# GFNet mixing and SoLU on one core: the opening's first step in the place of x, unit 0 from SBUF to SBUF, the tables' issues in another order

## The chip, the core and the metric

The program runs on one core of a Trainium2 chip. A core has a matrix engine (PE, with its weight loads shown as PEld), a vector engine (DVE), a scalar engine (ACT), a general engine (POOL) and a sequencer that only issues transfers and waits (SP). Transfers (DMAs) are issued by SP, ACT or POOL and carried by 16 DMA engines between DRAM and the on-chip memory (SBUF, 128 partitions). Products land in PSUM. The metric is the time of one execution on the device in microseconds (us).

## What is computed

The reference has two parts. Eight samples of 3136 tokens with 256 channels are filtered along the tokens in the frequency domain, and the result goes through a gated layer:

```python
X = np.fft.rfft(x, axis=1)
Y = X * (filt_r + 1j * filt_i)[None, :, :]
y = np.fft.irfft(Y, n=3136, axis=1)            # (8, 3136, 256)
h = y.reshape(25088, 256) @ w_in               # (25088, 1024)
sm = softmax(h); solu = h * sm                 # with 1e-9 in the denominator
ln = (solu - mean) / sqrt(var + 1e-6) * g_ln
out = ln @ w_out                               # (25088, 256)
```

The weights w_in and w_out arrive as 64-bit floats and are converted on the chip.

## The kernel before, in words

**The transform.** 3136 = 49 x 64. A sample goes through four steps. The *first step* (`Spectrum.first`, L204) multiplies x, as 98 rows (49 rows and their mirror images) by 32 positions by 256 channels, with a table of 98 x 100: 8 pieces of 4 positions, four matmuls each, copied out of PSUM by ACT (L213) and stored to DRAM (`d1`, L166 and L167: 96 rows on one queue, the last 4 rows on the other). The 100 result rows are 25 residues by 4 parts. The *forward step* (`forward`, L242) takes them back with residues along the free axis: 7 units of four residues (two pairs), the last of one. `fetch` (L226, L229) reads a unit of 512 KB from d1. Per unit PE makes `pb`, DVE multiplies with the filter (`multiply`, L260 to L262: two products and a sum for the real part on DVE, two products on DVE and the sum on POOL for the imaginary part), PE makes `pc` (`inverse`, L267), ACT copies it to `g` (L277) and `store` (L281) puts it to DRAM (`d2`). The *back step* (`fetch_back`, `back`, L285 to L304) reads d2 in 8 pieces `t4`, multiplies (`py`) and copies to `y`, which holds two samples' worth of tokens.

**The opening** (L307 to L490) does sample 0 alone and converts the weights. Its pools are: `fp` for the tables and filters, `t1` (two buffers of 4 KB in each partition), `r` (32 KB, one buffer: all of x of sample 0, later all of t4), `t2` (two of 4 KB), `p`, `g` and `wp` (raw weights, three of 4 KB, and `power`, two of 2 KB). Results of the first step go to t1 for pieces 0 and 1 and to spare places in `y` for pieces 2 to 7; units 1 to 6 are later fetched to the same spare places, unit 0 to t2. `load_tables(i0, n, dma)` (L361) issues nine transfers: a table `de` (L363) and eight parts of the filters `f` (L366). `begin(j)` (L391, L316) issues the load of raw weights j of 8, on POOL. `idle` (L426) is a matmul whose result nobody reads; eight of them stand in PE's order between the first step and the first forward step, and they read the first tables and filters.

**The conversion** (`load_float64`, L321) of one eighth of the weights: DVE makes eight instructions (L328 to L341), ACT one multiply (L330), POOL a product and a sum (L342, L343).

**What sets the order.** Within a `manual_schedule` block each engine works in the order in which the program emits its instructions. The opening is one such block and the main loop another; instructions emitted outside them (the x loads of the second sample's pieces 6 and 7, L776, called at L813) are placed by the scheduler when their memory is free. Before the change the opening's issues are: SP: x pieces 0 to 7 of the first half (one, one, two, two, two pieces at a time, row 48 apart), the four-row stores, fetches of units 0 to 2, tables of pairs 4 to 7, fetches of units 3 and 4, tables of pairs 8 to 12, fetches of units 5 and 6, then t4, x of the second sample, and the filters' copy to DRAM (L478). POOL: the second half of x, raw weights 0 and 1, tables of pairs 0 to 3, then its halves of conversions 0 and 1. ACT: the stores of the first step and of the units.

**After the opening** new pools take the memory of the opening's pools from the same start: wk2 (36 KB), fp1 (8), up (22), hp (16), wk (5), sp (4), r1 (12: x and t4 of later samples), t1 (6), t2, p, g, de1. The main loop (L819, `step`) runs over 196 blocks of 128 tokens: products with w_in, softmax, layer norm, transposes, products with w_out, and between them the transforms of samples 1 to 7, whose first steps store to d1 with L217 on POOL's queue.

The lines that the change moves, as they stood:

```python
fetch_x(0, n0, n, 0, N1 - 1, nc.sync.dma_start)             # L414
sp.first(i, (0, 1), ps_h.tile(...), nc.scalar.copy,
         None if i < 2 else spare_piece(i - 2)[0:NK])       # L422
sp.fetch(i, nc.sync.dma_start, spare_piece(i - 1) if i >= 1 else None)   # L450
convert(j)                                                  # L482
```

Of the kernel before, what the change touches and what calls it, by code (L numbers as in the profile page):

```python
# [9 lines left out]
FP32 = mybir.dt.float32  # L10
I32 = mybir.dt.int32
AFT = mybir.ActivationFunctionType
ALU = mybir.AluOpType
# [4 lines left out]
P = 128  # L18
B, S, C = 8, 3136, 256
# [4 lines left out]
N1, N2 = 49, 64  # L24
NH = N2 // 2
NS, NQ = (N1 + 1) // 2, 64
NP = (NS + 1) // 2
NR = 2 * N1
NK = 4 * NS
NCH = 4  # L30
KD, KF = C // P, DFF // P
# [57 lines left out]
def kernel(  # L89
# [10 lines left out]
    nc = tc.nc  # L100
# [5 lines left out]
    def pool(name, bufs, space=None, stack=ctx):  # L106
        kw = {} if space is None else {"space": space}
        return stack.enter_context(tc.tile_pool(name=name, bufs=bufs, **kw))
# [14 lines left out]
    w_in_sb = consts.tile([P, 7, DFF // 2], FP32, name="w_in_sb")  # L123
# [8 lines left out]
    def weight_sums(w):  # L132

        for to, a, b in ((3, 6, 0), (5, 2, 6), (4, 2, 3), (6, 1, 4)):
            nc.vector.tensor_tensor(out=w[:, to], in0=w[:, a], in1=w[:, b], op=ALU.subtract)
# [33 lines left out]
    class Spectrum:  # L169
# [24 lines left out]
        def fetch_x(self, i, halves, out=None):  # L194
            if out is None:
                out = self.pools["r"].tile([P, NCH, C], FP32, name=f"x_{self.e}_{i}", tag="r")
            self.xs[i] = out
            xb = x[self.e]
            for h, first, step in ((0, NCH * i, C), (1, N2 - 1 - NCH * i, -C)):
                halves[h](out[N1 * h:N1 * h + N1],  # L200
                          bass.AP(tensor=xb.tensor, offset=xb.offset + first * C,
                                  ap=[[N2 * C, N1], [step, NCH], [1, C]]))
# [91 lines left out]
    def back(e, ch, cb, evac):  # L294

        ps = ps_t.tile([P, 512], FP32, name=f"py_{e}_{ch}_{cb}", tag="t")

        psv = ps[:, 0:NCH * NR].rearrange("p (m r) -> p m r", r=N1)
        for i in range(NCH):
            nc.tensor.matmul(out=psv[:, i:2 * NCH - i:2 * NCH - 1 - 2 * i, :],  # L300
                             lhsT=t4s[e, ch][:, i, cb * P:cb * P + P], rhs=wi_t, start=True, stop=True)
        t0, last = e % 2 * S, N2 // NCH - 1
        evac(out=y[:, cb, t0:t0 + S].rearrange("p (r m j) -> p m j r", m=N2 // NCH, j=NCH)[  # L303
            :, ch:last + 1 - ch:last - 2 * ch], in_=psv.rearrange("p (m j) r -> p m j r", m=2))  # L304


    with ExitStack() as st:  # L307
        fpool = pool("fp", 1, stack=st)
        pools = {name: pool(name + "0", bufs, stack=st)
                 for name, bufs in (("t1", 2), ("r", 1), ("t2", 2), ("p", 2), ("g", 2))}  # L310
        wpool = pool("wp", 3, stack=st)
        ps_h = pool("ps_h", 3, PSUM, stack=st)

# [7 lines left out]
        def load_float64(dst, raw, negate=False):  # L321


            lo, hi = raw[:, :, 0], raw[:, :, 1]
            power = wpool.tile([P, 512], I32, name="power", tag="power", bufs=2)
            frac = dst.bitcast(I32)
            ts, stt = nc.vector.tensor_scalar, nc.vector.scalar_tensor_tensor
            ts(out=lo, in0=lo, scalar1=8, scalar2=None, op0=ALU.logical_shift_right)  # L328
            rest = lo.bitcast(FP32)
            nc.scalar.mul(rest, lo, 2.0 ** -44)  # L330
            ts(out=power, in0=hi, scalar1=20, scalar2=0x7FF, op0=ALU.logical_shift_right,
               op1=ALU.bitwise_and)
            ts(out=power, in0=power, scalar1=896.0, scalar2=0.0, op0=ALU.subtract, op1=ALU.max)
            ts(out=power, in0=power, scalar1=255.0, scalar2=None, op0=ALU.min)
            ts(out=power, in0=power, scalar1=23, scalar2=-2 ** 31 if negate else 0,
               op0=ALU.logical_shift_left, op1=ALU.bitwise_or)
            stt(out=power, in0=hi, scalar=-2 ** 31, in1=power, op0=ALU.bitwise_and,
                op1=ALU.bitwise_xor)
            ts(out=frac, in0=hi, scalar1=0xFFFFF, scalar2=3, op0=ALU.bitwise_and,
               op1=ALU.logical_shift_left)  # L340
            nc.vector.tensor_tensor(out=frac, in0=frac, in1=power, op=ALU.bitwise_or)  # L341
            nc.gpsimd.tensor_tensor(out=rest, in0=rest, in1=power.bitcast(FP32), op=ALU.mult)  # L342
            nc.gpsimd.tensor_tensor(out=dst, in0=dst, in1=rest, op=ALU.add)  # L343

        filters, tables = {}, {}

# [5 lines left out]
        def spare_piece(i):  # L352
            return spare[i % 2][:, i // 2 * NCH * C:(i // 2 + 1) * NCH * C].rearrange(
                "p (n c) -> p n c", c=C)
# [6 lines left out]
        def load_tables(i0, n, dma):  # L361
            de = fpool.tile([P, n, 2, 2, NQ], FP32, name=f"de_{i0}", tag=f"de{i0}")
            dma(out=de, in_=de_dram[i0:i0 + n].rearrange("i p k u q -> p i (k u q)"))  # L363
            f = fpool.tile([P, n, 2, C], FP32, name=f"f_{i0}", tag=f"f{i0}")
            for place, k, held, rows in all_filter_rows(i0, n):
                dma(out=f[place, 0:held, k, :], in_=rows)  # L366
            for i in range(n):
                tables[i0 + i], filters[i0 + i] = (de, i), (f, i)

        weights = []  # L370
# [17 lines left out]
        sp = Spectrum(0, pools, resident(filters), resident(tables))  # L388
        raws = {}

        def begin(j):  # L391
            raws[j] = load_words(weights[j][1], j)
# [5 lines left out]
        rows_x = pools["r"].tile([P, NH, C], FP32, name="x_0", tag="r")  # L398
# [10 lines left out]
        pieces = NH // NCH  # L409

        fetch_x(0, 0, NCH, 0, N1 - 1, nc.sync.dma_start)
        fetch_x(0, 0, NH, N1 - 1, 1, nc.sync.dma_start)
        for n0, n in ((NCH, NCH), (2 * NCH, 2 * NCH), (4 * NCH, 2 * NCH), (6 * NCH, 2 * NCH)):
            fetch_x(0, n0, n, 0, N1 - 1, nc.sync.dma_start)  # L414
        for n0, n in ((0, NCH), (NCH, NCH), (2 * NCH, 2 * NCH), (4 * NCH, 2 * NCH), (6 * NCH, 2 * NCH)):
            fetch_x(1, n0, n, 0, N1, nc.gpsimd.dma_start)
        for j in range(2):
            begin(j)
        load_tables(0, 4, nc.gpsimd.dma_start)
        for i in range(pieces):  # L420
            sp.xs[i] = rows_x[:, NCH * i:NCH * i + NCH]
            sp.first(i, (0, 1), ps_h.tile([P, 2, 512], FP32, name=f"pa_0_{i}", tag="h"),  # L422
                     nc.scalar.copy, None if i < 2 else spare_piece(i - 2)[0:NK])
            sp.store_first(i, 0, lambda out, in_: by_16((nc.scalar.dma_start, nc.sync.dma_start), out, in_))

        def idle(out):  # L426
# [8 lines left out]
        idle_row(8, "idle")  # L435

        def convert(j):
            load_float64(weights[j][0], raws.pop(j), negate=j < 4)

        for j in range(2):  # L440
            convert(j)

        def start(i):
            sp.fetch_filter(i)
# [1 line left out]
            sp.forward(i, halves(f"pb_0_{i}"))  # L446

        units = len(sp.units)
        for i in range(units):
            sp.fetch(i, nc.sync.dma_start, spare_piece(i - 1) if i >= 1 else None)  # L450
            if i in (2, 4):
                load_tables(2 * i, 4 if i == 2 else NP - 8, nc.sync.dma_start)
        for i in range(2):
            start(i)
        for i in range(units):
# [20 lines left out]
        for i0, n, rows in ((0, 4, P), (4, 4, P), (8, NP - 9, P), (NP - 1, 1, NQ)):  # L476
            f, at = filters[i0]
            nc.sync.dma_start(  # L478
                out=f_dram[i0:i0 + n].rearrange("i u q k c -> (u q) i (k c)")[0:rows],
                in_=f[0:rows, at:at + n].rearrange("p i k c -> p i (k c)"))  # L480
        for j in range(2, 8):
            convert(j)  # L482
            if j < 5:
                begin(j + 3)
            if j == 4:
                weight_sums(w_in_sb)
            if j > 2:
                for ch in {3: (0, 1), 4: (2, 3), 5: (4, 5), 6: (6, 7), 7: ()}[j]:
                    for cb in range(KD):
                        back(0, ch, cb, nc.scalar.copy)  # L490


    ps_b = [pool(f"ps_b{u}", 1, PSUM) for u in range(2)]
# [12 lines left out]
    pools = dict(f=pool("fp1", 2))  # L506
# [105 lines left out]
    def h_half(k, i):  # L612
        return hs[k][:, 512 * i:512 * i + 512]
# [7 lines left out]
    def finish(j, k, i, kept, bank):  # L621


        if k not in nmaxs:
            nmaxs[k] = small.tile([P, 2], FP32, name=f"nmax_{k}", tag=f"nmax{k % 2}")
            sofar, to = 3.0e38, nmaxs[k][:, 0:1]
        else:
            sofar, to = nmaxs[k][:, 0:1], nmaxs[k][:, 1:2]
        if kept is None:
            nc.vector.tensor_scalar(out=h_half(k, i), in0=ms[j, bank], scalar1=0.0, scalar2=sofar,  # L630
                                    op0=ALU.add, op1=ALU.min, accum_out=to)
        else:
            nc.vector.tensor_tensor_reduce(out=h_half(k, i), in0=ms[j, bank], in1=h_half(*kept),  # L633
                                           scale=1.0, scalar=sofar, op0=ALU.add, op1=ALU.min,
                                           accum_out=to)
# [131 lines left out]
    for e in range(1, B):  # L767
        first_at, spectrum_at, back_at = PLAN[e]
        sp = Spectrum(e, pools, load_filter, load_de)
        if e == 1:  # L770
            sp = second
# [172 lines left out]
```

## Time and profile before

| what | value |
|---|---|
| median of 6 runs | 1723.05 us (1718.37 to 1724.25) |
| the profiled execution | 1718.37 us, span 1716.6 us |
| busy share of the span | PE 95%, DVE 71%, POOL 64%, ACT 55% |
| mean granted PE clock | 0.979 |
| DMA, whole span | 180 GB/s mean |
| 0 to 39 us | PE busy 20.8 us, DVE 7.5, DMA share 0.93 |
| 39 to 49 us | PE busy 9.9 us, DVE 0, DMA share 0.72 |
| 49 to 84.3 us | PE busy 21.7 us, DVE 21.2, DMA share 0.79 |
| 84.3 to 107 us | PE busy 18.3 us, DVE 22.1, DMA share 0.91 |
| 107 to 126 us | PE busy 16.5 us, DVE 15.9, clock 0.59 |
| 126 to 172 us | PE busy 38.7 us, DVE 18.7, clock 0.86 |
| 172 to 1700 us | PE busy 1497.6 us of 1528, clock 0.99 |

The profile is of one execution. The span runs from the first to the last instruction. A row of a timeline gives start, duration, engine, line, operation, output and inputs, and in brackets the idle time of the engine before it and what ended it. The chain of waits is followed back from the last instruction: at each step to what released it. A transfer in the chain, such as "DMA d<-g", lasts from its issue to the moment when what waited for it went on. Names are the program's tile names: x, t (t1, t2 and t4), y, pa, pb, pr, pi, pt, pc, g, d (d1 and d2), de, f, raw, power. SPq and ACTq are issues of transfers or waits on those engines.

### The profile page before, as it was taken

Reading aid. Unit: us, or ns where it says so; the run is one execution under the profiler, and the core shown is the slowest. Engines: PE = TensorE matmul, PEld = TensorE weight load, DVE = VectorE, ACT = ScalarE, POOL = GpSimd, SP = SyncE. Lnnn points to the kernel's source line nnn. Section 1 sums busy time; section 2 is a strip of 40 time slices with the busy share of each in tenths; the row PEclk is TensorE's granted clock in tenths of the full one; section 3 lists DMA queues with packets and bytes.
Section 4 is the critical chain, followed back from the end, with each engine's and each line's share of the span. In section 5 each row is a group of like instructions: output and inputs, shape, how many; then the busy total and the mean of one; then the engine's idle time right before and its main releaser. Section 6 shows DMA issues by size and latency. Waiting matters only on the chain.

```text
span 1716.6 us, 30283 instructions
## 1 busy us (share of the span) xinstructions
PE 1632.8 (95%) x9816; PEld 1119.9 (65%) x9816; DVE 1219.1 (71%) x2583; ACT 945.2 (55%) x1734; POOL 1091.2 (64%) x1307
## 2 busy tenths in 40 slices
PE   5688899899999999999999999999999999999997
PEld 1353356667666666666677666776777777777766
DVE  1593677577777787678767788668877776777782
ACT  2144555555556555655566555664666566656552
POOL 3254786556766676667676666756566665667664
PEclk9878899999999999999999999999999999999999
DMA  8886878667786677668875776568754454444443
GB/s 217 252 248 192 261 220 251 187 171 184 232 246 190 169 234 229 172 158 222 233 187 135 199 219 195 156 156 212 214 143 103 121 127 117 114 104 107 113 103 101
DMA packets 368001, 308.71 MB, mean 180 GB/s; under 512 B 63466, under 2 KB 334211, under 8 KB 367699
## 3 DMA queue, kind: packets, MB, share of 16 engines
q1 hardware_dynamic: 289316, 149.42, 34.1%
q0 software_dynamic: 42016, 119.33, 23.6%
q10 hardware_dynamic: 36512, 38.02, 7.5%
q8 instruction: 80, 1.31, 0.3%
q14 instruction: 77, 0.63, 0.1%
HBM read 122.34 MB, written 81.50 MB: 119 GB/s over the span
## 4 chain that ended last, share of the span: by engine, by line
PE 77%; DMA 8%; DVE 8%; issue 2%; ACT 2%; POOL 2%; SPq 1%; ACTq 0%; DVEq 0%; POOLq 0%
PE o L721 31%; PE m L609 30%; PE py L300 6%; PE pa L211 5%; DMA de<-de_tbl 3%; PE pb L239 3%; PE pc L239 2%; DVE h L657 2%; DMA d<-t 1%; DMA solu_t<-turn 1%; SPq L679 1%; DMA t<-d 1%; DVE pt L261 1%; ACT e L641 1%; PE idle L428 1%
## 5 line engine op out<-in xcount | busy, mean ns | idle before, releaser
L659 ACT ACTIVATE e<-h,nmu 128x1024 f32<-128x1024 f32 x196 | 225.4, 1150 | 334.4 <-DVE h L657 333.0
L721 PE MATMUL o<-w_out_sb,solu_t 128*128 128x128 f32 x3136 | 401.7, 277 | 4.0 <-DVE ot L738 1.9
L721 PEld LDWEIGHTS o<-w_out_sb,solu_t 128*128 128x128 f32 x3136 | 379.4, 193 | 35.6 <-issue 28.3
L721 PEld LDWEIGHTS o<-w_out_sb,u 128*128 128x128 f32 x2352 | 307.1, 192 | 143.7 <-issue 113.3
L609 PE MATMUL m<-w_in_sb,s 128*128 128x512 f32 x784 | 399.2, 600 | 0.9 <-ACT h L619 0.9
L587 POOL TENSOR_TENSOR u<-solu_t 128x512 f32<-128x512 f32 x98 | 149.7, 1527 | 283.8 <-DMA solu_t<-turn 159.1
L721 PE MATMUL o<-w_out_sb,u 128*128 128x128 f32 x2352 | 312.4, 276 | 5.3 <-ACT ot L733 4.1
L609 PE MATMUL m<-w_in_sb,y 128*128 128x512 f32 x588 | 309.0, 609 | 5.7 <-DVE nmax L633 4.3
L657 DVE SCALAR_TENSOR_TENSOR h<-e,rsum,h 128x1024 f32<-128x1024 f32 x196 | 281.7, 1437 | 6.9
L740 DVE SCALAR_TENSOR_TENSOR ot<-o,rs_t,ot 128x128 f32<-128x128 f32 x294 | 102.5, 349 | 245.6 <-ACT ot L733 205.1
L667 DVE STREAM_TRANSPOSE turn<-h 128x1024 f32<-128x1024 f32 x196 | 242.4, 1237 | 1.6 <-DMA solu_t<-turn 0.4
L619 ACT COPY h<-m 128x512 f32<-128x512 f32 x294 | 172.4, 586 | 123.2 <-PE m L609 118.9
L641 ACT ACTIVATE e<-h,nmax 128x1024 f32<-128x1024 f32 x196 | 225.0, 1148 | 0.0
L633 DVE CUSTOM_DVE_ANT_0 h<-m,h 128x512 f32<-128x512 f32 x196 | 134.3, 685 | 112.1 <-ACT h L619 79.4
L587 POOL TENSOR_TENSOR u<-solu_t,u 128x512 f32<-128x512 f32 x98 | 139.6, 1424 | 90.8 <-PE o L721 86.7
L609 PEld LDWEIGHTS m<-w_in_sb,s 128*128 128x128 f32 x784 | 131.0, 192 | 86.0 <-issue 77.6
L300 PEld LDWEIGHTS py<-wi_t,t 100*128 100x128 f32 x1024 | 135.1, 199 | 50.4 <-issue 38.4
L609 PEld LDWEIGHTS m<-w_in_sb,y 128*128 128x128 f32 x588 | 99.2, 194 | 80.9 <-issue 50.8
L587 POOL TENSOR_TENSOR solu_t<-solu_t,solu_t 128x512 f32<-128x512 f32 x98 | 145.6, 1485 | 7.7
L300 PE MATMUL py<-wi_t,t 100*128 100x98 f32 x1024 | 137.0, 281 | 12.4 <-DMA t<-d 9.7
L303 ACT COPY y<-py 128x392 f32<-128x392 f32 x128 | 108.1, 846 | 66.3 <-PE py L300 65.5
L211 PE MATMUL pa<-x,wf_t 98*100 98x512 f32 x232 | 129.8, 654 | 14.5 <-DMA x<-in_x_dram 13.8
(96 smaller groups left out, 1919.4 us busy)
## 6 DMA issues: line engine op xcount, KB each, us to landing
solu_t<-turn SPq DMA_DIRECT2D x784, 128.0 KB
out_dram<-ot SPq DMA_DIRECT2D x196, 128.0 KB
d<-t POOLq DMA_DIRECT2D x112, 200.0 KB, 4.8
t<-d POOLq DMA_DIRECT2D x56, 400.0 KB, 5.1
x<-in_x_dram POOLq DMA_DIRECT2D x102, 196.0 KB, 5.6
f<-f_dram POOLq DMA_DIRECT2D x39, 512.0 KB, 6.7
d<-g POOLq DMA_DIRECT2D x39, 512.0 KB, 5.6
t<-d ACTq DMA_DIRECT2D x36, 512.0 KB
```

Source lines behind the costliest of these rows:

```text
L211: nc.tensor.matmul(out=ps[0:NK, j], lhsT=wf_t, rhs=self.xs[i][0:NR, 2 * u:2 * u + 2, :], start=True, stop=True)
L300: nc.tensor.matmul(out=psv[:, i:2 * NCH - i:2 * NCH - 1 - 2 * i, :], lhsT=t4s[e, ch][:, i, cb * P:cb * P + P], rhs=wi_t, start=True, stop= ...
L303: evac(out=y[:, cb, t0:t0 + S].rearrange("p (r m j) -> p m j r", m=N2 // NCH, j=NCH)[:, ch:last + 1 - ch:last - 2 * ch], in_=psv.rearrange ...
L587: nc.gpsimd.tensor_tensor(out=out, in0=in0, in1=in1, op=op)
L609: nc.tensor.matmul(out=ms[j, bank], lhsT=lhsT, rhs=w_in_sb[:, w, :], start=m in (1, 2, 7), stop=True, skip_group_check=True)
L619: nc.scalar.copy(out=h_half(k, i), in_=ms[j, 0])
L633: nc.vector.tensor_tensor_reduce(out=h_half(k, i), in0=ms[j, bank], in1=h_half(*kept), scale=1.0, scalar=sofar, op0=ALU.add, op1=ALU.min, ...
L641: nc.scalar.activation(out=e, in_=hs[k], func=AFT.Exp, bias=nmaxs.pop(k)[:, 1:2], scale=-1.0, accum_out=esum)
L657: nc.vector.scalar_tensor_tensor(out=solu, in0=e, scalar=rsum, in1=solu, op0=ALU.mult, op1=ALU.mult, accum_out=nmu)
L659: nc.scalar.activation(out=e, in_=solu, func=AFT.Square, bias=nmu, scale=-float(DFF), accum_out=variances[g][:, i:i + 1])
L667: nc.vector.transpose(out=turns[g][:, :, i, :], in_=solus.pop(k).rearrange("p (f j) -> p f j", j=32))
L721: nc.tensor.matmul(out=pos[p, bank], lhsT=lhs[:, f, :], rhs=w[:, f, :], start=f == 0 and m in (1, 2, 7), stop=True, skip_group_check=True)
```

## The change

- The pool t1 goes, and t2 has one buffer. The first step's result is written where the piece of x stood, in rows 0 to 99 of the x tile.
- x of sample 0 is loaded piece by piece in both halves: eight transfers on SP besides row 48, eight on POOL. Raw weights 0 are begun on POOL after piece 4, raw weights 1 after piece 7.
- Tables and filters of pairs 4 to 7 are issued on POOL right behind those of pairs 0 to 3; before, SP issued them after fetch 2. SP issues the tables of pairs 8 to 12 after fetch 2; before, after fetch 4.
- Unit 0 is not fetched from d1. Sixteen transfers from SBUF to SBUF copy rows 0 to 15 of the first step's result, each one partition of 32 KB, to 32 partitions of 1 KB each; they alternate between SP and ACT.
- `load_float64` returns a function that emits ACT's multiply and POOL's two operations. In conversions 3 to 7 it is called after the next piece of program has been emitted; DVE's part of conversion j + 1 is emitted behind the last parts of conversion j.

```diff
-                 for name, bufs in (("t1", 2), ("r", 1), ("t2", 2), ("p", 2), ("g", 2))}
+                 for name, bufs in (("r", 1), ("t2", 1), ("p", 2), ("g", 2))}
...
-            nc.scalar.mul(rest, lo, 2.0 ** -44)
...
-            nc.gpsimd.tensor_tensor(out=rest, in0=rest, in1=power.bitcast(FP32), op=ALU.mult)
-            nc.gpsimd.tensor_tensor(out=dst, in0=dst, in1=rest, op=ALU.add)
+
+            def finish():
+                nc.scalar.mul(rest, lo, 2.0 ** -44)
+                nc.gpsimd.tensor_tensor(out=rest, in0=rest, in1=power.bitcast(FP32), op=ALU.mult)
+                nc.gpsimd.tensor_tensor(out=dst, in0=dst, in1=rest, op=ALU.add)
+
+            return finish
...
-        for n0, n in ((NCH, NCH), (2 * NCH, 2 * NCH), (4 * NCH, 2 * NCH), (6 * NCH, 2 * NCH)):
-            fetch_x(0, n0, n, 0, N1 - 1, nc.sync.dma_start)
-        for n0, n in ((0, NCH), (NCH, NCH), (2 * NCH, 2 * NCH), (4 * NCH, 2 * NCH), (6 * NCH, 2 * NCH)):
-            fetch_x(1, n0, n, 0, N1, nc.gpsimd.dma_start)
-        for j in range(2):
-            begin(j)
+        for i in range(pieces):
+            if i:
+                fetch_x(0, NCH * i, NCH, 0, N1 - 1, nc.sync.dma_start)
+            fetch_x(1, NCH * i, NCH, 0, N1, nc.gpsimd.dma_start)
+            if i in (4, 7):
+                begin(i // 7)
         load_tables(0, 4, nc.gpsimd.dma_start)
+        load_tables(4, 4, nc.gpsimd.dma_start)
         for i in range(pieces):
             sp.xs[i] = rows_x[:, NCH * i:NCH * i + NCH]
+
             sp.first(i, (0, 1), ps_h.tile([P, 2, 512], FP32, name=f"pa_0_{i}", tag="h"),
-                     nc.scalar.copy, None if i < 2 else spare_piece(i - 2)[0:NK])
+                     nc.scalar.copy, sp.xs[i][0:NK])
...
-            load_float64(weights[j][0], raws.pop(j), negate=j < 4)
+            return load_float64(weights[j][0], raws.pop(j), negate=j < 4)
 
         for j in range(2):
-            convert(j)
+            convert(j)()
...
-        for i in range(units):
-            sp.fetch(i, nc.sync.dma_start, spare_piece(i - 1) if i >= 1 else None)
-            if i in (2, 4):
-                load_tables(2 * i, 4 if i == 2 else NP - 8, nc.sync.dma_start)
+
+        sp.t2s[0] = t2_0 = pools["t2"].tile([P, 4, C], FP32, name="t2_0_0", tag="t2")
+        for n in range(16):
+            (nc.sync, nc.scalar)[n % 2].dma_start(
+                out=t2_0[NH * (n % 4):NH * (n % 4) + NH, n // 4, :], in_=rows_x[n:n + 1])
+        for i in range(1, units):
+            sp.fetch(i, nc.sync.dma_start, spare_piece(i - 1))
+            if i == 2:
+                load_tables(8, NP - 8, nc.sync.dma_start)
...
-        for j in range(2, 8):
-            convert(j)
-            if j < 5:
-                begin(j + 3)
-            if j == 4:
-                weight_sums(w_in_sb)
-            if j > 2:
-                for ch in {3: (0, 1), 4: (2, 3), 5: (4, 5), 6: (6, 7), 7: ()}[j]:
-                    for cb in range(KD):
-                        back(0, ch, cb, nc.scalar.copy)
+
+        rest = {2: convert(2)}
+        rest.pop(2)()
+        begin(5)
+        rest[3] = convert(3)
+        for ch in range(pieces):
+            if ch in (0, 2, 4, 6):
+                j = 3 + ch // 2
+                rest.pop(j)()
+                if j < 5:
+                    begin(j + 3)
+                rest[j + 1] = convert(j + 1)
+                if j == 3:
+                    weight_sums(w_in_sb)
+            for cb in range(KD):
+                back(0, ch, cb, nc.scalar.copy)
+        rest.pop(7)()
```

## The prediction

> **What bounds the kernel now.** I read the page first: PE is busy 95% of the span, and its digits show that the loop over token blocks is full while the first slices are not. The change edits only what comes before that loop, so I went through the chain that ended last from 0 to 200 us, then the issues of SP, the rows of POOL and the rows of DVE there. The loop's work after the opening is unchanged and nothing in it is tied to a time of day, so I count a microsecond taken off the chain in the opening as a microsecond of the whole. From the chain, window 30 to 135 us (start us, us, what):
>
> ```profile
> 32.53 6.16 DMA f<-in_filt_i_dram
> 38.82 2.06 PE idle L428 x2
> ...
> 43.05 5.68 PE idle L428 x12
> 48.73 1.12 PE pb L239 x16
> ...
> 56.70 5.19 DMA d<-g
> 61.91 3.20 DMA f<-in_filt_r_dram
> 65.12 8.42 DMA y<-d
> 73.68 2.01 PE pb L239 x16
> ...
> 123.78 1.29 POOL w_out_sb L343
> 125.09 0.59 ACT t L213
> 125.97 6.56 DMA d<-t
> ```
>
> The reader is to see four links. The filters of pairs 0 to 3 land at 38.7 and start the eight idle products; these end at 48.7 and only then does unit 0's forward step (pb) run. Then a filter issue on SP waits for the store of unit 0's result (d<-g) to land at 61.9. Behind it on SP stand the fetches of units 5 and 6, so unit 5's forward step comes at 73.7. Last, the second sample's first copy (ACT t) waits for the last POOL operation of the last conversion, at 125.07. What the second and third link cost is on DVE (timeline of DVE; in brackets the idle time and what ended it):
>
> ```profile
> 59.24 0.68 DVE L260 TENSOR_TENSOR pr<-pb,f 128x512 f32<-128x512 f32 x1
> 65.83 0.69 DVE L260 TENSOR_TENSOR pr<-pb,f 128x512 f32<-128x512 f32 x1 [3.33 <-DMA f<-in_filt_r_dram]
> 71.38 0.69 DVE L261 TENSOR_TENSOR pt<-pb,f 128x512 f32<-128x512 f32 x1 [4.86 <-DMA f<-in_filt_i_dram]
> 78.81 0.69 DVE L260 TENSOR_TENSOR pr<-pb,f 128x512 f32<-128x512 f32 x1 [4.82 <-PE pc L239]
> 84.31 0.41 DVE L328 TENSOR_SCALAR raw<-raw 128x512 int32<-128x512 int32 x1
> ```
>
> DVE multiplies units 0 to 3 from 49.87 to 62.5 at 3.1 us each without a pause, then stands for 3.33 + 4.86 + 4.82 = 13.0 us, and begins conversion 2 at 84.31. From there to 106 the chain is DVE's conversions.
>
> **How many transfers are in flight.** POOL's filter issues stand at 11.42, 16.19, 21.52 us, each released by the landing of an x transfer, exactly eight issues before it. SP and ACT share eight such places in turn: SP's waits have the row "SPq L366 <- DMA d<-g", 8.3 us, once. An issue that has no data to do with d<-g waits because the transfer eight places before it was that store.
>
> **Part 1, x in pieces of one step.** Issues: SP 9 rather than 6, POOL 8 rather than 5, at 0.3 to 0.6 and 0.87 us, all while the first bytes travel; nothing. On POOL 512 KB of raw weights now stands ahead of x pieces 5 to 7, so the last piece has the 2.0 MB ahead of it that raw 0 had before: it lands when raw 0 did, 28.4 us (DVE's first row, 28.41, waits for it). Four products at 0.43 and the copy at 1.0 us put the end of the first step at 31 to 32 us if PE is warm, 35.5 (today's) if not. That gain of 0 to 4 us is hidden: the idle products wait for filters that have the same bytes ahead of them on POOL as before, so 38.8 stays, within 1 us.
>
> **Part 2, unit 0 from SBUF.** Removed: one fetch of 512 KB (SP, 0.40 us). Added: 16 copies of 32 KB, eight on SP and eight on ACT, some 0.4 us per issue. They are not free of the DRAM stores: with eight places in turn, copies 0 to 7 wait for the stores of pieces 4 to 7 to land, and copies 8 to 15 for copies 0 to 7. The last store lands at 40.7 today (SP's first fetch follows at 40.85), so the copies take two rounds after at most 40.7. No row shows a copy out of one partition. From below: the loop's regrouping from SBUF to SBUF (128 KB, L679 at 184.69) lands 2.6 us after its issue, so two rounds end at 40.7 + 5.2 = 46. From above: all 512 KB through one DMA engine in 1 KB packets, which take 46 ns each in the trace, 512 x 46 ns = 23.6 us, ending at 62 to 65. I take 46, because the regrouping is the nearest row. It is covered: idle products hold PE until 48.7. So no gain from this part either, and no loss up to 2.7 us of lateness; beyond that each microsecond counts in full. SP's fetch 1 moves behind the eight copies, from 41.30 to some 43.5, landing near 47; unit 1's forward step is due at 49.8.
>
> The Trainium skill, "SBUF — State Buffer", Door 1, speaks against this part: partitions 0 to 15 reach four of sixteen ports, so by its 436 GB/s the 512 KB would take 4.8 us, an estimate. No run here shows it, and it too would fit under the idle products. "DMA: Bandwidth & Descriptors", on why a semaphore goes up by 16, has the engine count follow from the outer sizes, here 32 and 32, hence 16 engines. What the trace has on a single partition is the load of x row 48 (32 KB in one run), which posted one completion, 4.7 us after its issue.
>
> **Part 3, filters of pairs 4 to 7 on POOL.** Nine issues leave SP (42.39 to 50.0: 7.6 us with waits) and go behind the first filters on POOL. The last of them goes out near 41, so the POOL halves of conversions 0 and 1 (4 x 1.28 us, today 36.7 to 41.9) end near 47; POOL's next work is due at 53.17, so that is hidden. The DMA engines stand at 0.72 of their share from 39 to 49, and this fills it. On SP the order is now fetch 1, 2, then the nine issues for pairs 8 to 12, then fetches 3 to 6: fifteen issues at 0.4 to 0.5 us from 43.5. The later ones wait for landings eight places before, at 46 to 50, so fetch 3 goes out near 50 and fetch 6 near 52, where fetch 5 goes out at 65.12 today. They land by 54 to 58; units 3, 4, 5 are due at 55.5, 59.8, 63. The pairs 8 to 12 are due at 62.5 and land near 54. The store of unit 0 (56.7) now comes after SP's last table issue, so nothing that DVE needs waits for it. All three DVE pauses go: conversion 2 begins at 84.3 - 13.0 = 71.3. **-13.0 us.** What is late next is DVE itself (7 units at 3.1 us).
>
> **Part 4, conversions' last parts.** I wrote out each engine's order for both versions: ACT has mul 2, mul 3, copies of pieces 0 and 1, mul 4, copies 2 and 3, and so on in both; POOL, DVE and PE also keep theirs. An ACT multiply needs only the shift (L328), emitted before it in both. Nothing, with 1 us either way for what I overlook: the conversions then shift as a block.
>
> **Part 5, what the memory plan moves.** The pools lie one behind another and are reused by later pools. Without t1 and with one t2 buffer the opening's pools are 12 KB shorter, and by the sizes in the code the main loop's x buffers (12 KB, pool r1), which lay on products and results of the opening, now lie 8 KB deep on the converters' buffers. The x loads of the second sample's pieces 6 and 7 go out at 95.15 to 99.27 today (POOL, 0.60 + 0.79 + 0.55 + 0.78 = 2.7 us). I expect them to wait, as ACT t does today, for the last POOL operation of conversion 7: in today's times 125.1. There they stand ahead of the first store d<-t, which is on the chain, by 2.7 us less its idle wait of 0.9, that is 1.8 us, and with 784 KB in the same queue. Three d<-t stores of 200 KB need 6.56 us there, but the conversions' stretch is freed of the same bytes. From both sides: 0 (the scheduler puts the stores first) to 7 us; I take **+3**, near the 1.8 of issue that is sure if they stand in front. Their own data are due at 140.8 (PE pa<-x), and even 10 to 15 us of landing, as today, is in time.
>
> **Sum.** -13.0 + 3 = -10 against the profiled execution of 1718.4 us (span 1716.6): 1708. It is the fastest of the six; their median, 1723.05, lies 4.7 above it, so I forecast 1713 for the median.
>
> **Rivals.** (a) *A store still stands in the turn.* If the fetch of unit 4 or 5 is eight places behind unit 0's store, it goes out at 62 and lands at 66 to 68, against a need of 59.8 to 63; DVE then pauses some 5 us. For it: that is today's pattern. Against: only fetches 3 to 6 follow. -13 + 5 + 3 = -5: 1718. (b) *Nothing to pay in the plan of memory, and filters 1 to 3 us sooner*, if fewer waits on SP and POOL help: -13 to -16: 1708. (c) *Slower: the 16 copies run on one engine one after another.* They end at 62 to 65 rather than 46, unit 0 begins 13 to 17 us late, and DVE's 21 us of units then start there: +14 to +17 - 13 + 3 = +4 to +7, 1727 to 1730. It decides once the copies land later than 48.7 + 10 = 59. Speaking for it: the one-partition load that had one completion. Against: the copies have 32 rows on the other side. (d) *It doesn't do what it says:* the idle products, the filters in front of them and DVE's conversions set the pace whatever is fetched, and the r1 loads cost 7: the sum is within 0.2%.
>
> **How the numbers follow.** Forecast 46% (1709 to 1717), (a) 16%, (b) 13%, (c) 17%, (d) 8%. 0.2%, 3.4 us, is about what a measurement of this kernel tells from no change. Faster: the forecast, (b) and most of (a), 0.70; same: the rest of (a), (d) and a little of (c), 0.14; slower 0.16. The range leaves out the lowest of (b) and nearly all of (c): 1706 to 1725.
>
> **What would show it.** Right: no bracket on DVE's L260 and L261 rows between unit 0 and conversion 2, conversion 2 at 70 to 73; pb of unit 0 still within 1.5 us of 48.7 and right behind the idle products; the second sample's x loads behind the last L343. Wrong: "DMA t<-x" ahead of the first pb; an SP fetch released by d<-g; conversion 2 later than 78.

## The result and the profile after

The changed kernel takes 1716.10 us (median of 23 runs, 1707.14 to 1722.39); the kernel before, beside it on the same chips, 1722.87 us (48 runs). The ratio is 0.9963, with a 95% interval of 0.9953 to 0.9973: 6.4 us faster (4.7 to 8.1). Its profiled execution took 1713.52 us, with a span of 1711.7 us, against 1718.37 and 1716.6 before.

The chain of waits in the changed kernel from 27 to 121 us (start us, us, what):

```profile
26.96 3.60 DMA d<-x
...
31.89 6.72 DMA t<-x
38.63 5.97 DMA t<-x
...
45.99 7.32 DMA f<-in_filt_r_dram
53.33 6.62 DMA y<-d
60.08 2.01 PE pb L239 x16
62.09 2.00 PE pc L434 x2
64.09 1.59 PE pc L239 x16
...
116.05 1.35 POOL w_out_sb L345
117.69 2.79 POOL x L794 x4
120.48 7.26 DMA d<-t
```

The eight idle products ahead of unit 0 and the store of unit 0 (d<-g) have left the chain. In their place stand the last stores of the first step, two rounds of SBUF-to-SBUF copies (t<-x), one filter transfer and fetch 3 (y<-d), which sets off unit 3's forward step at 60.08. Further on, the four x loads on POOL (L794) stand between the last conversion and the first store d<-t, as the prediction had it.

The timeline of DVE in the changed kernel (in brackets the idle time before the row and what ended it), and that of SP:

```profile
47.43 0.69 DVE L260 TENSOR_TENSOR pr<-pb,f 128x512 f32<-128x512 f32 x1 [15.90 <-PE pb L239]
65.71 0.69 DVE L260 TENSOR_TENSOR pr<-pb,f 128x512 f32<-128x512 f32 x1 [8.83 <-PE pc L239]
77.53 0.41 DVE L328 TENSOR_SCALAR raw<-raw 128x512 int32<-128x512 int32 x1
```

```profile
30.59 11.00 SPq L458 DMA_DIRECT2D t<-x  x8
42.49 1.88 SPq L229 DMA_DIRECT2D y<-d  x2
...
45.02 2.85 SPq L370 DMA_DIRECT2D f<-in_filt_r_dram  x4
47.91 5.07 SPq L370 DMA_DIRECT2D f<-in_filt_i_dram  x4
53.33 7.65 SPq L229 DMA_DIRECT2D y<-d  x4
```

Three pauses of 13.0 us have become one of 8.83 us, and conversion 2 begins at 77.53 rather than at 84.31. The four fetches 3 to 6 leave SP from 53.33 on, behind the eight issues of filters for pairs 8 to 12.

The row at 65.71 is unit 3's first, and it waits for a product pc, not for its own pb. By the code, DVE's products have two buffers, so unit 3's take the place of unit 1's once PE has made unit 1's pc from them, and that pc stands in PE's order behind unit 3's pb. The operands of that pc were ready at 55.1 us, where POOL's sum ends, but PE stood until fetch 3 had landed, then made pb, idle products for 2.00 us (L434) and only then pc. So 3.6 of the 8.83 us follow unit 3's pb. None of the kernels below has another order on PE.

The stretches from 35 to 45 us show what became of the transfers. The columns are the window, its length, the busy times of PE, PEld, DVE, ACT and POOL, PE's granted clock, the DMA engines' mean busy share and GB/s. First the kernel before:

```profile
35.00:40.00 5.00, 1.18 (x2) 0.50 (x2) 1.17 (x3) 1.69 (x3) 3.26 (x3) 0.68 0.58 208
40.00:45.00 5.00, 4.88 (x8) 1.57 (x7) 0.00 (x0) 0.00 (x0) 1.83 (x2) 0.64 0.55 189
```

Then the changed kernel:

```profile
35.00:40.00 5.00, 4.09 (x4) 1.00 (x4) 0.00 (x0) 0.00 (x0) 1.89 (x5) 0.50 1.02 244
40.00:45.00 5.00, 4.94 (x11) 2.30 (x11) 0.00 (x0) 0.00 (x0) 4.74 (x5) 0.87 0.91 191
```

The DMA engines that stood half idle are full: (0.44 + 0.36) x 5 us = 4.0 us of DMA time were filled. But the rate hardly rose (208 and 189 to 244 and 191 GB/s): the engines are now busy with something that takes long for its bytes.

### The profile page after: what moved, and what is told of

The parts are those of the page before. It is cut to its first block, busy times and chain, and to the rows that moved or that the text cites. A ratio compares the mean times of both kernels' runs of the same rounds, so it can differ in the third digit from the quotient of the medians.

```text
span 1711.7 us, 30324 instructions
## 1 busy us (share of the span) xinstructions
PE 1627.4 (95%) x9816; PEld 1119.8 (65%) x9816; DVE 1213.2 (71%) x2583; ACT 945.6 (55%) x1734; POOL 1097.8 (64%) x1319
## 4 chain that ended last, share of the span: by engine, by line
PE 74%; DMA 11%; DVE 8%; POOL 2%; issue 2%; ACT 2%; SPq 1%; ACTq 0%; DVEq 0%; POOLq 0%
PE o L739 29%; PE m L627 29%; PE pa L211 5%; PE py L300 5%; PE pb L239 3%; DMA solu_t<-turn 2%; DVE h L675 2%; PE pc L239 2%; DMA t<-d 2%; DMA de<-de_tbl 1%; DMA x<-in_x_dram 1%; DMA d<-t 1%; DMA t<-x 1%; DMA d<-x 1%; DVE pt L261 1%
## 5 line engine op out<-in xcount | busy, mean ns | idle before, releaser
L675 DVE SCALAR_TENSOR_TENSOR h<-e,rsum,h 128x1024 f32<-128x1024 f32 x196 | 277.6, 1417 | 6.9
L211 PE MATMUL pa<-x,wf_t 98*100 98x512 f32 x232 | 124.6, 630 | 11.6 <-DMA x<-in_x_dram 10.0
```

The lines of the kernel that those rows point to most:

```text
L211: nc.tensor.matmul(out=ps[0:NK, j], lhsT=wf_t, rhs=self.xs[i][0:NR, 2 * u:2 * u + 2, :], start=True, stop=True)
L675: nc.vector.scalar_tensor_tensor(out=solu, in0=e, scalar=rsum, in1=solu, op0=ALU.mult, op1=ALU.mult, accum_out=nmu)
```

## The experiments

Times are given against the kernel before, run beside each on the same chip: the ratio with its 95% interval. One trace of each kernel shows where it went. Three executions of the changed opening (its own trace, a repetition, and the kernel with the old memory plan, which has the same order on PE, DVE and ACT) begin conversion 2 at 77.53, 78.77 and 75.62, so a single trace is good to some 1.6 us there.

**My theory** after the first comparison: the gain is the shorter pause of DVE, and it is held down by SP's queue, in which the copies and then the filters of pairs 8 to 12 stand ahead of fetch 3. **Rivals:** the DMA engines are full from 30 to 60 us and only bytes count; or the gain comes from the earlier x.

### Unit 0 from DRAM again

```
-for n in range(16): (nc.sync, nc.scalar)[n % 2].dma_start(out=t2_0[...], in_=rows_x[n:n + 1])
+sp.fetch(0, nc.sync.dma_start)
```

> The changed kernel, but unit 0's rows are fetched from DRAM by one transfer of 512 KB on SP again; everything else stays changed. Theory (the queue of issues): in the changed kernel the sixteen copies hold SP back, fetch 1 goes out at 42.5 us and fetch 3 at 53.3, and DVE stands for 8.8 us behind it; without the copies fetch 0 goes out when the last store of the first step has landed (35.0 us), fetch 1 and 2 right behind, and fetch 3 before 48. DVE's pause of 8.8 us goes, conversion 2 begins near 69 to 71 rather than at 77.5, and the time is 5 to 9 us below the changed kernel. Rival (the bytes): the DMA engines are busy 0.94 to 0.97 of the time from 30 to 60 us whoever issues, the same 512 KB now cross from DRAM, fetch 3 still lands near 60: within 2 us of the changed kernel. Second rival (the copies are worth their place): unit 0 lands later than the idle products end (46.0) and the time is 2 to 5 us above the changed kernel.

Measured: 1712.32 us, ratio 0.9945 (0.9924 to 0.9967). DVE's rows:

```profile
61.75 0.69 DVE L260 TENSOR_TENSOR pr<-pb,f 128x512 f32<-128x512 f32 x1 [4.71 <-PE pc L239]
73.59 0.41 DVE L328 TENSOR_SCALAR raw<-raw 128x512 int32<-128x512 int32 x1
```

The fetches 0 to 2 went out from 35.82 on, yet fetch 3 only at 50.83: the filters' issues, from 38.70 to 50.60, waited for landings themselves. Conversion 2 begins 3.9 us sooner than in the changed kernel's trace, 2.0 sooner than the earliest of the three. Unit 0 from DRAM was not late (DVE begins at 47.59, against 47.43). By the traces the copies cost time: my theory had the sign and overstated the size, and the second rival is out. The first rival (only the bytes count, within 2 us) is not: the two ratios are 3.1 us apart, and their intervals overlap.

### Filters of pairs 4 to 7 back on SP

```
-load_tables(4, 4, nc.gpsimd.dma_start)
-    if i == 2: load_tables(8, NP - 8, nc.sync.dma_start)
+    if i in (2, 4): load_tables(2 * i, 4 if i == 2 else NP - 8, nc.sync.dma_start)
```

> The changed kernel, but the filters of pairs 4 to 7 are issued by SP again, behind fetch 2, and those of pairs 8 to 12 behind fetch 4, as before the change. Theory (this move is what the change gains): the pauses of DVE return, some 13 us or more in place of 8.8, because nine more issues stand ahead of fetches 5 and 6 and meet the store of unit 0's result; conversion 2 begins 4 to 9 us later than 77.5 and the time is 4 to 9 us above the changed kernel, about that of the kernel before. Rival (the gain comes from the earlier x): the loss is under 2 us, since fetch 3 stands behind nine issues in both.

Measured: 1722.78 us, ratio 1.0010 (0.9993 to 1.0027): the whole gain is gone. DVE:

```profile
69.45 0.69 DVE L260 TENSOR_TENSOR pr<-pb,f 128x512 f32<-128x512 f32 x1 [8.05 <-DMA f<-in_filt_r_dram]
71.28 0.69 DVE L261 TENSOR_TENSOR pt<-pb,f 128x512 f32<-128x512 f32 x1 [1.13 <-DMA f<-in_filt_i_dram]
79.10 0.69 DVE L260 TENSOR_TENSOR pr<-pb,f 128x512 f32<-128x512 f32 x1 [5.21 <-PE pc L239]
```

The three pauses of before are back, 14.4 us of them, and the chain runs through d<-g (55.84, 7.69 us) as it did before the change.

### The memory plan of before

```
-("t2", 1)
+("t2", 4)
```

> The changed kernel with four buffers in pool t2 rather than one (the three others are never used), so that the main loop's x buffers lie where they lay before the change and no longer on the converters' buffers. Theory (part 5 of the prediction, with the 2.79 us that the four x issues take on POOL ahead of the first d<-t in the changed kernel): the four x loads go out before 100 us, the first d<-t right behind the first ACT t copy, and the time is 2 to 3 us below the changed kernel. Rival: their 784 KB now compete with the raw weights of conversions 6 and 7 or with the second sample's rows, and the time is within 1 us of the changed kernel.

Measured: 1713.59 us, ratio 0.9961 (0.9943 to 0.9979), the changed kernel's own. POOL's rows:

```profile
115.06 1.28 POOL L345 TENSOR_TENSOR w_out_sb<-w_out_sb,raw 128x512 f32<-128x512 f32 x1
117.26 1.17 POOL L217 DMA_DIRECT2D d<-t  x2 [0.91 <-ACT t L213]
```

The x loads have left that place, and from the last L345's end to the first d<-t it takes 0.92 us rather than 3.09. Those 2.2 us are real in the trace and can't be found in the time, whose interval is 3 us to either side.

### x in the pieces of before

The loop over single pieces is replaced by the two loops of before (4, 4, 8, 8, 8 positions, then the raw weights).

> The changed kernel, but x is loaded in the pieces of before (4, 4, 8, 8, 8 steps), all x before the first raw weights on both queues. Theory (a chain through the first step: x, stores of the first step, copies, SP's issues, fetch 3): the last store of the first step lands near 40.7 rather than 35.0, every later link shifts, and the time is 3 to 6 us above the changed kernel. Rival (as the prediction put it: the filters of pairs 0 to 3 set the start of unit 0 whatever x does): the idle products start within 1 us of the changed kernel's, and the time is within 1.5 us of it.

Measured: 1720.71 us, ratio 0.9992 (0.9977 to 1.0008). DVE begins unit 0 at 58.12 and conversion 2 at 81.17; the chain is the changed kernel's, 7 to 10 us later (a copy from 39.20 to 49.12, the next to 53.72). The idle products start at 37.88 rather than 35.85, so the rival is out. With the copies in place, the early x is worth 5 us: the stores wait for it and the copies for the stores.

### Filters alone, on the kernel before

```
+load_tables(4, 4, nc.gpsimd.dma_start)
-    if i in (2, 4): load_tables(2 * i, 4 if i == 2 else NP - 8, nc.sync.dma_start)
+    if i == 2: load_tables(8, NP - 8, nc.sync.dma_start)
```

> The kernel before with one part of the change alone: the filters of pairs 4 to 7 are issued by POOL behind those of pairs 0 to 3, and SP issues those of pairs 8 to 12 behind fetch 2. Theory (the prediction's part 3, which no sixteen copies hold up here): fetch 3 goes out near 50 to 52 us, DVE's three pauses of 13.0 us shrink to 5 or less, conversion 2 begins at 73 to 77 rather than at 84.3, and the time is 7 to 11 us below the kernel before. Rival (the queue is full whatever the order, and the change needs x in pieces as well, since the changed kernel with x as before is as slow as the kernel before): within 3 us of the kernel before.

Measured: 1717.69 us, ratio 0.9974 (0.9957 to 0.9990), 4.5 us faster. Fetch 3 goes out at 51.91, the pauses shrink to one of 5.09 us, conversion 2 begins at 74.64:

```profile
62.82 0.69 DVE L260 TENSOR_TENSOR pr<-pb,f 128x512 f32<-128x512 f32 x1 [5.09 <-PE pc L239]
74.64 0.41 DVE L328 TENSOR_SCALAR raw<-raw 128x512 int32<-128x512 int32 x1
```

The opening did nearly as the theory said; the time gained, 4.5 us (1.7 to 7.4), lies below its 7 to 11 and above the rival's 3. The interval overlaps the changed kernel's: what all other parts together add to this one, these times can't tell from nothing.

### Fetches ahead of the last filters

```
-    if i == 2: load_tables(8, NP - 8, nc.sync.dma_start)
+    if i == units - 1: load_tables(8, NP - 8, nc.sync.dma_start)
```

> The changed kernel with one move: SP issues the fetches 3 to 6 ahead of the filters of pairs 8 to 12, not behind them. Theory (fetch 3 is late because it stands in the queue behind nine issues, each of which waits for the landing eight places before it): fetch 3 goes out at 44 to 45 us rather than 53.3, DVE's pause of 8.83 us shrinks to under 2, conversion 2 begins at 69 to 72 rather than 77.5, and the time is 5 to 8 us below the changed kernel. Rival (the DMA engines are full from 30 to 60 us, and what is taken from one transfer is given to another): the filters of pairs 8 and 9, due at 60 us, are now the late ones, a pause of 5 to 9 us stands ahead of unit 4, and the time is within 3 us of the changed kernel.

Measured: 1716.93 us, ratio 0.9975 (0.9955 to 0.9994): no better than the changed kernel. DVE:

```profile
66.55 0.69 DVE L261 TENSOR_TENSOR pt<-pb,f 128x512 f32<-128x512 f32 x1 [5.09 <-DMA f<-in_filt_i_dram]
74.61 0.41 DVE L328 TENSOR_SCALAR raw<-raw 128x512 int32<-128x512 int32 x1
```

Fetch 3 left before 45 and landed in time, and the pause went to unit 4, whose filters landed at 66.3. My theory falls, and by the time the rival holds (conversion 2 begins 2.9 us sooner in the trace, 1.0 sooner than the earliest of the three). Its reason, the full DMA engines, is not the whole of it. The chain has, ahead of the late filter:

```profile
55.08 6.70 DMA d<-g
...
62.15 4.18 DMA f<-in_filt_i_dram
```

The last two filter issues waited on SP for the store of unit 0's result to land, 4.5 us, as the filter issue at 61.91 did before the change. An estimate from these rows: without that wait the pause of 5.09 us would be about 1 or less. So a store in the turn made these filters late; that it landed late itself (6.70 us, against 5.19 before) may be the full engines' part.

### All copies on ACT

```
-(nc.sync, nc.scalar)[n % 2].dma_start(
+nc.scalar.dma_start(
```

> The changed kernel with all sixteen copies issued by ACT, none by SP. Theory (SP and ACT share eight places in turn, in the order of the program, so it doesn't matter which of the two issues): fetch 1 still goes out at 42 us or later, fetch 3 at 53 or later, and the time is within 2 us of the changed kernel, or up to 3 above it, as one engine must issue sixteen copies in a row. Rival (the copies stand in SP's own queue): fetch 1 goes out at 36 us, fetch 3 near 50, as in the kernel without copies, and the time is 3 to 5 us below the changed kernel.

Measured: 1716.68 us, ratio 0.9963 (0.9946 to 0.9980). SP's queue:

```profile
36.77 0.99 SPq L229 DMA_DIRECT2D y<-d  x2
44.21 0.36 SPq L367 DMA_DIRECT2D de<-de_tbl  x1
...
53.59 2.08 SPq L229 DMA_DIRECT2D y<-d  x4
```

Fetch 1 went out 5.7 us sooner, against the theory, and the next issue still waited until 44.21, for fetch 1 to land, and fetch 3 went out at 53.59, against the rival. The last copy was issued at 49.16 and DVE began unit 0 at 54.47, with no pause behind it; conversion 2 came at 75.70. For the time it doesn't matter who issues.

### Nothing moved for unit 0

```
-for n in range(16): ...
+sp.t2s[0] = filters[0][0][:, 0:2].rearrange("p i k c -> p (i k) c")
```

> The changed kernel without the sixteen copies and without any fetch in their place: unit 0 multiplies rows of the first filters, which lie in SBUF already, so this kernel leaves the regrouping of unit 0's rows out of the computation. It has 512 KB and sixteen issues less than the changed kernel, and 512 KB and one issue less than the kernel whose unit 0 comes from DRAM (conversion 2 at 73.59 there, 77.53 in the changed kernel). Theory (the DMA engines are full, so a transfer costs its bytes, by whatever way it goes): 512 KB at the 240 to 260 GB/s of 30 to 60 us are 2.0 to 2.2 us, so conversion 2 begins at 71 to 72 and the time is 5 to 6 us below the changed kernel. Rival (only the issues count, each waiting for the landing eight places before): as with one fetch from DRAM, conversion 2 at 73 to 74, the time 3 to 4 us below the changed kernel.

Measured: 1710.45 us, ratio 0.9931 (0.9905 to 0.9956). DVE:

```profile
58.88 0.69 DVE L260 TENSOR_TENSOR pr<-pb,f 128x512 f32<-128x512 f32 x1 [2.53 <-PE pc L239]
70.70 0.41 DVE L328 TENSOR_SCALAR raw<-raw 128x512 int32<-128x512 int32 x1
```

The time is 5.5 us below the changed kernel by the two ratios, as the theory had it, but its reason fails: the way does matter. In the opening, unit 0's rows from DRAM cost 73.59 - 70.70 = 2.9 us, and the sixteen copies 77.53 - 70.70 = 6.8 (4.9 to 8.1 with the three executions). The packets give a likely reason. In the trace of the kernel with all copies on ACT, whose queue then carries nothing else of this size, the 512 packets of 1 KB took 132 ns each on their DMA engine (mean; median 69, one in ten over 440); in the changed kernel and its repetition ACT's half of them took 134 and 201 ns. The packets of 1 KB that SP's fetches and filters moved from DRAM in the kernel whose unit 0 comes from DRAM took some 60 ns (mean; median 46 to 58, by the stretch taken). So 512 copies' packets fill sixteen engines for 512 x 132 ns / 16 = 4.2 us, and the same bytes from DRAM for 2.0 us. The difference of 2.3 to 4.5 us (from 132 and 201 ns) is of the size by which the traces differ (2.0 to 5.2 us). Trace by trace the two don't go together: with the memory plan of before the packets took 164 ns, and conversion 2 came soonest of the three. And sixteen issues in the turn instead of one are a rival that no kernel here tries by itself. What is left of the pause, 2.53 us, is PE's order: the last fetch needed landed at 53.9, pb ended at 56.1, and idle products and pc fill the rest.

### x in pieces alone, on the kernel before

The loop over single pieces, and nothing else of the change.

> The kernel before with one part of the change alone: x in pieces of one step on both queues, the raw weights behind pieces 4 and 7. Theory (x is ahead of all that follows on the DMA engines; its last store lands some 5 us sooner, SP's fetches and tables go out that much sooner, and the filters of pairs 0 to 3 land at 35.5 rather than 38.7): unit 0's products start some 3 us sooner, so its store lands sooner, and with it the issues behind it; conversion 2 begins 2 to 5 us before 84.3 and the time is 2 to 5 us below the kernel before. Rival (as the prediction put it: hidden, because the pauses of DVE behind the store of unit 0 are not touched): within 1.5 us of the kernel before.

Measured: 1718.85 us beside 1719.95, ratio 0.9993 (0.9975 to 1.0012): nothing. Its one trace begins conversion 2 at 79.19, 5 us sooner than before, which the twelve times don't confirm. By the time, this part alone is hidden; by the trace it isn't. I leave that open.

### Two versions that take more

The first fetches unit 0 from DRAM, puts the fetches ahead of the filters of pairs 8 to 12 and keeps the old memory plan.

> The changed kernel with three edits: unit 0 fetched from DRAM by one transfer, fetches 3 to 6 ahead of the filters of pairs 8 to 12, and the four t2 buffers that put the main loop's x buffers back in their old place. Theory: all seven fetches go out from 35.8 to 41 us and land before 50, the filters of pairs 8 to 12 land before 58, DVE's 21.6 us of units run from 47.6 without a pause, conversion 2 begins at 69 to 70, and the time is 8 to 12 us below the changed kernel, 14 to 18 below the kernel before. Rival (the filters of pairs 8 and 9 become late, or conversion 2 waits for its raw weights): 4 to 6 us below the changed kernel, as without the copies alone.

Measured: 1711.62 us, ratio 0.9941 (0.9919 to 0.9964). A pause of 3.00 us ahead of unit 4's filters remains, and conversion 2 begins at 72.54. That is the rival's case: by the two ratios (0.9941 and 0.9963) it is 3.8 us below the changed kernel, just short of the rival's 4 to 6. Again the last filter issue waited on SP for d<-g, until 59.86 us (4.4 us).

The second puts the weight sums one conversion later as well:

```
-                if j == 3:
+                if j == 4:
                     weight_sums(w_in_sb)
```

> The kernel with unit 0 fetched from DRAM, the fetches ahead of the filters of pairs 8 to 12 and the old memory plan, and one edit more: the weight sums of w_in (four DVE operations, 2.91 + 0.69 us) stand behind conversion 5 on DVE rather than ahead of it. Theory: in the changed kernel ACT's multiply of conversion 5 waits for its shift behind these sums, and the copies of pieces 4 and 5 stand behind that multiply on ACT, idle for 3.49 us; with the sums later they start 3 us sooner, the second sample's first copy too as far as DVE's conversion 7 allows, and the time is 2 to 3 us below the same kernel with the sums in their place, 12 to 14 us below the kernel before. Rival (DVE's conversions are the longer chain): within 1 us of the same kernel with the sums in their place.

Measured: 1708.70 us, ratio 0.9930 (0.9909 to 0.9950). ACT's one wait for a shift (4.43 us in the version without this edit) has become two, of 2.14 and 2.66, and from conversion 2 to the last L345 it takes 41.0 us as against 40.9: by the trace DVE's conversions are the longer chain, as the rival said. The time is 1.9 us below the first version's by the ratios, and the two intervals overlap; both versions beat the kernel before, and the second the changed kernel too.

### The changed kernel again

> The changed kernel, unaltered, beside the three others on one chip, so that their times can be set against it directly. All theories: 0.995 to 0.9975 of the kernel before; conversion 2 within 1.5 us of 77.5, with DVE's pause ahead of unit 2 between 7.5 and 10 us, unless that pause depends on which transfers happen to land first.

Measured: 1716.19 us, ratio 0.9970 (0.9952 to 0.9987), beside the second version's 1708.70 on the same chip. Conversion 2 begins at 78.77, with a pause of 7.27 us, shorter than expected. DVE begins unit 0 at 50.22 here, and at 50.05 in the kernel with the old memory plan, against 47.43 in the changed kernel's own trace.

## Why the prediction was right, and where it was not

The forecast was 1713 us, the time is 1716.1: faster, within the range, somewhat over half the way towards rival (a). The sum of -10 us stands against 6.4 us (4.7 to 8.1). The range, 1706 to 1725, also holds the kernel before (1722.87), so lying inside it says less than the direction does.

**By its own signs** the account behind the number held only in part. Of the signs of being right, two came: the x loads stand behind the last conversion, and unit 0's pb right behind the idle products. But a pause stayed on DVE (8.83 us), conversion 2 began at 77.53 and not by 73, and unit 0's pb at 46.0 and not within 1.5 us of 48.7. Of the signs of being wrong, an SP fetch released by d<-g came (fetch 6), and in the kernel with the old memory plan unit 0's pb waited for copies. Step by step:

**Part 1, x (0, hidden).** Two readings failed. Raw 0 landed at 20.0 us, the last x at 24.8 and not at 28.4, and the last store at 34.4 where it had been 40.7. And "38.8 stays" was wrong: the filters of pairs 0 to 3 landed at 35.55. I had counted bytes ahead of each transfer and taken the rate as fixed; from 20 to 30 us it rose from 323 to 404 GB/s at the same busy share of 1.02. That this part alone saves nothing fits the time of the kernel that has it alone (0.9993), if not its trace. Beside the copies it isn't nothing: the changed kernel without it loses 5 us (0.9992), nearly its whole gain, as the copies wait for the stores and the stores for x.

**Part 2, copies (0).** The copies ended at 46.7 (46 predicted) and fetch 1 went out at 42.49 (43.5), but that was luck. I read 2.6 us off the regrouping at 184.69, which in the trace lands 5.0 us after its issue, and a copy took 3.5 to 8.2 us. Two rounds so slow end at 46.7 only because they began at 30.2 and not at 40.7; in the two other executions they end at 49.3. The price was wrong. I looked for it in unit 0's lateness alone, and there none was (DVE begins at 47.43; 50.1 and 50.2 in the others, which the later pause takes up). By the traces it lies in the transfers behind: "the DMA engines stand at 0.72 of their share from 39 to 49, and this fills it" priced the free room once and spent it on the filters and the copies both. Leaving the copies out for a fetch makes conversion 2 come 3.9 us sooner. In time the two kernels' intervals (0.9945 and 0.9963) overlap, so the price is shown in the traces and only likely in the time. It fits that the four kernels without copies lie at 0.9930 to 0.9945 (two of them with further edits), and the five with copies, the filters on POOL and x in pieces at 0.9961 to 0.9975.

The Trainium skill, "SBUF — State Buffer", Door 1, was cited against this part: few source partitions reach few ports, an estimate of 4.8 us. The packets' 4.2 us, an estimate, agree in sign and size; that ports are the reason, no run here shows.

**Part 3, filters (-13).** This is the step that failed in size. The mechanism held: without it the whole gain is gone (1.0010), and alone it brings 4.5 us (1.7 to 7.4). But fetch 3 went out at 53.33 rather than near 50 and landed at 59.9 rather than by 55.5, when it was due. I counted issues and the landings eight places before; I did not ask when the bytes would be through. From 35 to 55 us the share is 0.91 to 1.02, and landings took long: 7.32 us for the filter part that released fetch 3, 6.62 us for fetch 3. How much of that is full engines and how much the turn, the runs don't separate. Nor is a place always the one of eight issues before. The filter issue of before at 61.91 waited for a store issued at 56.70, only two issues ahead of it among SP's and ACT's; the two post to the same semaphore, one of eight that both engines use in the trace. The pause left was 8.83 us; the two links together gave 84.31 - 77.53 = 6.8 us, not 13.

**Part 4, conversions (0).** Right, by the traces: ACT's multiplies and copies stand in the same order, and from conversion 2 to the last sum on POOL it takes 40.8 us before and 39.9 after. No kernel has it by itself.

**Part 5, plan of memory (+3).** The rows came as described: four loads, 2.80 us on POOL, ahead of d<-t. Put back, they free 2.2 us of the chain in the trace and nothing that the time can show.

**Rivals.** (a) was near in size and wrong in place: fetch 6 did wait 5.0 us for d<-g on SP, but unit 6 is due last, and the pause came from fetch 3. With the fetches first its mechanism does show, at the last filters. (c), the copies one after another, is out: they landed from 35 to 47 us. (b), at 1708, and (d) are out by the interval.

**From opening to whole.** The first product with w_out begins 5.9 us sooner in the trace after, and the span is 4.9 us shorter. The rule that a microsecond of the opening is one of the whole holds within 1 us in this pair of traces: between 319 and 358 us the trace of before makes up 1.8 us, where a transfer t<-d that PE waits for took 6.58 us and in the trace after 7.50. It is looser elsewhere: for the kernel with the filters alone the opening shows 9.6 us at that product, its span 3.3 and the time 4.5. The trace of before is one execution, the fastest of its six.

## What to carry to other kernels

Before moving issues about, look at two things in that very stretch: the busy share of the DMA engines, and what each late issue waits for. Here the share was 0.55 to 0.58 from 35 to 45 us, and the filters put there gained; with it near 1, putting the fetches first only chose which unit was late, the more so as a store stood in the turn. Spend the free room once: two parts of a change that are each hidden under the same idle share are not hidden together. A copy that stays on the chip isn't cheaper for it; weigh its packets' time. And when a pause ends with a product, see what stands ahead of that product on its own engine: here 3.6 us did.

## What was not expected of the hardware

- A copy of 32 KB out of one partition into 32: its 1 KB packets took 132 to 201 ns (mean; medians 58 to 79), against some 60 ns for 1 KB packets from DRAM in the same stretch (medians 46 to 58). A minority of long packets, one in ten over 380 to 465 ns by the trace, makes most of the difference.
- At the same busy share, 1.02, the engines moved 404 GB/s from 20 to 30 us and 244 GB/s from 35 to 40: the share alone doesn't give the rate.
- The same opening in three executions (one with the old memory plan) began conversion 2 at 75.6, 77.5 and 78.8 us.
